# GpSimd in place of VectorE for the low parts of the normalized columns, in the first attention stage of the second layer

## The chip, the cores and the metric

The kernel runs on one core of one Trainium2 chip. The metric is the device time of one execution in microseconds (us). Before the change it is 1368.17 us, the median of 3 runs that lie between 1368.06 and 1368.76.

The engines are named as the profile names them: PE is TensorE (matmuls; PEld its weight loads), DVE is VectorE, ACT is ScalarE, POOL is GpSimd, SP is SyncE, whose queue issues the DMAs.

## The reference

Two blocks, attention and dense, are applied twice to `x` of 2048 rows and 640 columns, all in f32. The two layers use the same weights.

```python
x = x + A(layernorm(x)); x = x + B(layernorm(x))    # layer 1
x = x + A(layernorm(x)); x = x + B(layernorm(x))    # layer 2

def A(x):                       # 32 heads of 20 columns
    q, k, v = split(x @ wqkv)
    pq, pk = q @ w_phi, k @ w_phi                   # per head, 20 by 20
    phi_q = concat([softmax(pq), softmax(-pq)])     # 40 features per head
    phi_k = concat([softmax(pk), softmax(-pk)])
    kv, z = phi_k.T @ v, sum_rows(phi_k)            # per head
    return ((phi_q @ kv) / (phi_q @ z + 1e-6)) @ wo

def B(x):
    h = x @ w1 + b1
    return (h * tanh(softplus(h))) @ w2
```

## The kernel before

**Stages.** Each layer has three stages: `attend_first` (normalized rows to keys, values and queries, and the sums `kva` over all rows), `attend_second` (queries times sums, projection with `wo`), and `dense`. Each stage goes over 8 blocks (`NB`) of 256 rows (`BLK`). The change lies in `attend_first` of the second layer (`layer` is 1), about 713 to 916 us of the profiled execution.

**High and low parts.** A matmul operand is kept as two f32r tiles: the high part is a rounded copy that ScalarE makes, the low part is what the copy left out, source minus high part. Each product is three matmuls: high by high, high by low, low by high (`project_half`, L369 to L375). For the normalized columns the parts are `xth` and `xtl`, made in `Transposed.step` (L302): ScalarE copies (L316, recorded under L132), VectorE subtracts (L317). A block has 5 groups of 128 columns, made in three steps: two of 128x512 (two groups each), one of 128x256.

**Where the columns come from.** In the first layer they are transposed on TensorE into PSUM. In the second, the dense stage has written the normalized rows transposed to memory (`n2_d`); `load_turned` (L350) fetches them into three row tiles `xn` (a pool of 4) and `step` takes source and high part from SBUF.

**The loop of the stage.** For block b the order is keys, values and queries of its two 128-row tiles, k0, k1, v0, v1, q0, q1 (L545). The columns of block b+1 are fetched at the first of these and split at the last three (`nxt.step()`, L574). `features` (L386), for keys and queries, goes round the engines: ScalarE copies out of PSUM, VectorE takes maxima and minima (L400) and subtracts (L401, L403; L401 is GpSimd's for queries), ScalarE takes the exponential (L406), VectorE sums and inverts (L409, L410), GpSimd multiplies (L411). Features of keys go to TensorE (L448); those of queries are transposed by VectorE (L456) and written to memory (`e_d`, L460), which sets their tile `r` free; there are two such tiles, and GpSimd clears part of a tile at its start (L391). The projections share two PSUM tiles `mm`, which ScalarE's copies set free.

**What sets the order.** Outside the parts written by hand, a planner that simulates the program puts the instructions of each engine in order when the kernel is built. ScalarE's are chained in program order (`act`). Each engine runs its instructions in that order, and an instruction that waits holds up those behind it.

**The other users of `Transposed`** are the first layer's first stage, both second stages, and the dense stages; the columns of the second layer's block b0 are made by the dense stage before it (L866).

Of the kernel before, what the change touches and what calls it, by code (L numbers as in the profile page):

```python
# [8 lines left out]
F32 = mybir.dt.float32  # L9
F32R = mybir.dt.float32r  # L10
AF = mybir.ActivationFunctionType
ALU = mybir.AluOpType
# [32 lines left out]
def kernel(  # L45
# [13 lines left out]
    nc = tc.nc  # L59
# [11 lines left out]
    def one_tile():  # L71
        return psum.tile([P, 512], F32, tag="one", name="one", bufs=4)
# [38 lines left out]
    n2_d = [dram.tile([D, BLK], F32, name=f"n2_d{b}") for b in range(NB)]  # L111
# [14 lines left out]
    def act(*args, **kw):  # L126

        if last_act[0] is None or in_written[0]:
            ins = nc.scalar.activation(*args, **kw)
        else:  # L130
            with tc.issue_after(last_act[0]):
                ins = nc.scalar.activation(*args, **kw)  # L132
        last_act[0] = ins.ins
# [143 lines left out]
    def norm_stats(t, xt):  # L277

        bn = work.tile([P, 2, 6], F32, tag="bn", name="bn", bufs=2)
        for c in range(2):  # L280
            nc.vector.bn_stats(bn[:, c], xt[:, t, c * HC:(c + 1) * HC])
        mv = work.tile([P, 2], F32, tag="mv", name="mv", bufs=3)
        nc.vector.bn_aggr(mv, bn)
        return mv

    def norm_scale(b, mvs):

        ve = work.tile([P, BT], F32, tag="ve", name="ve", bufs=2)
        for t in range(BT):
            nc.gpsimd.tensor_scalar(ve[:, t:t + 1], mvs[t][:, 1:2], LN_EPS, 1.0, op0=ALU.add, op1=ALU.mult)  # L290
        nc.gpsimd.tensor_tensor(stats[:, b, 0], ve, neg_half, op=ALU.pow)
        for t in range(BT):
            nc.vector.scalar_tensor_tensor(stats[:, b, 1, t:t + 1], mvs[t][:, 0:1], -1.0,
                                           stats[:, b, 0, t:t + 1], op0=ALU.mult, op1=ALU.mult)

    class Transposed:


        def __init__(self, rows=None, cols=None):
            self.rows, self.cols, self.hs, self.ls = rows, cols, [], []  # L300

        def step(self):  # L302
            c0 = len(self.hs)
            n = min(2, KD - c0)
            if self.rows is None:
                ps = self.cols[c0 // 2]
            else:
                ps = one_tile().rearrange("p (c s) -> p c s", c=2)
                for c in range(n):
                    for t in range(BT):  # L310
                        nc.tensor.transpose(ps[:, c, t * P:(t + 1) * P],  # L311
                                            self.rows[t][:, (c0 + c) * P:(c0 + c + 1) * P], ident)
            nb = 8 if n == 2 else 4
            hi = work.tile([P, n, BLK], F32R, tag=f"xt{n}", name="xth", bufs=nb)
            lo = work.tile([P, n, BLK], F32R, tag=f"xt{n}", name="xtl", bufs=nb)
            act(hi, ps[:, :n], AF.Copy)  # L316
            nc.vector.tensor_tensor(lo, ps[:, :n], hi.bitcast(F32), op=ALU.subtract)  # L317
            for c in range(n):
                self.hs.append(hi[:, c, :])
                self.ls.append(lo[:, c, :])  # L320
# [26 lines left out]
            for q in range(4):  # L347
                nc.sync.dma_start(dst[t, q], rows[t][32 * q:32 * q + 32].rearrange("f (j s) -> f j s", s=32))

    def load_turned(src, tiles):  # L350

        cols = []
        for c, make in zip(range(0, KD, 2), tiles):
            n = min(2, KD - c)
            cols.append(make()[:, :n * BLK].rearrange("p (k s) -> p k s", k=n))
            nc.sync.dma_start(cols[-1], src[c * P:(c + n) * P].rearrange("(k p) s -> p k s", p=P))
        return Transposed(cols=cols)


    def project(xts, t, ws, col, ps=None, w=HC):  # L360
# [53 lines left out]
    def fetch(x_src, b, xt=None):  # L414
        xt = x_tile() if xt is None else xt
        nc.sync.dma_start(xt, row_block(x_src, b))
        return xt

    def attend_first(layer, x_src, first):


        def fetch_normed(b):
            if layer:
                return load_turned(n2_d[b], [row_tile] * 3)
            xt = fetch(x_src, b) if b > 1 else early
            norm_scale(b, [norm_stats(t, xt) for t in range(BT)])
            return xt
# [50 lines left out]
        if first is None:  # L478
            with written():
# [48 lines left out]
                for k in range(KD):  # L528
                    ps = one_tile()
# [13 lines left out]
        for b in range(NB):  # L543
# [14 lines left out]
            for n, (kind, t) in enumerate(order):  # L558
                t = int(t)
                i = b * BT + t  # L560
                if b == 0 and n == (1 if layer else 3):
                    if layer == 0:
                        fold_phi(kv_ws, bd, raw)
                    kva = one_tile()
                    nc.vector.memset(kva[:, :360], 0.0)
                if b == NB - 1 and n == 3:
                    loaded = {0: load(0)}
                if b + 1 < NB:
                    if n == 0:
                        xt = fetch_normed(b + 1)  # L570
                    elif n == 2:
                        nxt = xt if layer else normed(b + 1, xt)
                    elif n > 2:
                        nxt.step()  # L574
                g = {"k": lambda: keys(xts, i, vs[t]), "q": lambda: queries(xts, i, q0 if i == 0 and not layer else None),
                     "v": lambda: values(xts, i, vs[t])}[kind]()
                next(g)
                advance()
                pending.append(g)
# [180 lines left out]
    def dense(x_src, x_dst, w1s, w2s, first, last):  # L760
# [97 lines left out]
        for i in range(len(steps) + SKEW):  # L858
            if i < len(steps):
                b, pr = steps[i]  # L860
                if pr == 0 and b + 1 < NB:
                    fetch_rows_of(b + 1)
                if pr == 2 and b + 1 < NB:
                    blocks[b + 1] = [fetch(x_src, b + 1), None, None]
                if pr == 3 and (b + 1 < NB or not last):
                    nxt = load_turned(n1_d[b + 1] if b + 1 < NB else n2_d[0], (v_tile, v_tile, row_tile))  # L866
                acts[i] = hidden(b, pr)
                if pr == 1 and b + 1 < NB:
                    with tc.issue_after(exps[0]):
                        normalize(b + 1, ahead, ahead)  # L870
                    spill_turned(ahead, n1_d[b + 1])
                if b == 0 and pr == n_pr - 2:
                    with tc.issue_after(exps[0]):
                        nxt.step()
                if pr == n_pr - 1 and (b + 1 < NB or not last):
                    if b + 1 < NB:
                        blocks[b + 1][1] = nxt
                    with tc.issue_after(exps[0]):
                        nxt.all()
# [15 lines left out]
    with tc.block(schedule_with_timeline_sim=True):  # L895
        src, first = x, None
        for layer in range(LAYERS):
# [41 lines left out]
            src = dst  # L939
# [38 lines left out]
```

## Time and profile before

| | us |
|---|---|
| median of 3 runs | 1368.17 |
| profiled execution | 1368.56 |
| its span | 1366.8 |
| PE busy | 1351.2 |
| DVE busy | 1075.5 |
| ACT busy | 578.4 |
| POOL busy | 452.6 |

The profile is of one execution, whose own time is 1368.56 us; its span, 1366.8 us, runs from the first to the last recorded work. In the rows of the timeline the first number is the start in us from the beginning of the span, the second the duration in us, then engine, line, operation and tiles; a bracket at the end gives the idle time of the engine before it and what ended it. In the groups by line, the number behind `x` is the count, then busy us and mean ns of one. In the list of waits stand total us, how often, and the longest. Issuing DMAs is not counted as busy.

### The profile page before, as it was taken

To read this page: it belongs to the slowest core of one execution; us is meant where nothing else is said; L and a number is where in the kernel's file an instruction comes from. 1 tells how busy PE (TensorE), PEld (TensorE's weight loads), DVE (VectorE), ACT (ScalarE), POOL (GpSimd) and SP (SyncE) were. 2 spreads that over 40 slices of the span, in tenths; PEclk is the share of its full clock that TensorE was granted. 3 is DMA by queue.
4 is the path that set the end of the run, shared out by engine and by line. 5 is a ranking of instruction groups with operands and counts; after the bars stand their busy time and mean duration, and the time that the engine had idled before them with its cause. 6 is when DMAs were issued, how large, how long until landed. Compare 5 with 4: busy or idle time off the path is not lost. (4 is left out here: it accounts for less than half of the span.)

```text
span 1366.8 us, 30959 instructions
## 1 busy us (share of the span) xinstructions
PE 1351.2 (99%) x12896; PEld 1337.9 (98%) x12896; DVE 1075.5 (79%) x1822; ACT 578.4 (42%) x970; POOL 452.6 (33%) x401
## 2 busy tenths in 40 slices
PE   9999999999999999999999999999999999999998
PEld 9999999999999999999999999999999999999998
DVE  6888988876787888778769898989668776677775
ACT  5444444212454544455444333432235444444443
POOL 2355554434222222122235444544252211111112
PEclk9999999999999999999999999999999999999999
DMA  9533333798714443334563433458974221333200
GB/s 343 150 81 64 74 60 78 213 282 273 223 36 93 116 117 84 57 94 113 151 218 75 83 60 70 86 132 267 287 251 136 78 71 35 90 97 97 77 21 20
DMA packets 350469, 169.19 MB, mean 124 GB/s; under 512 B 287209, under 2 KB 323801, under 8 KB 350329
## 3 DMA queue, kind: packets, MB, share of 16 engines
q1 hardware_dynamic: 350329, 167.22, 45.4%
q8 instruction: 101, 1.65, 0.5%
q14 instruction: 39, 0.32, 0.1%
HBM read 104.59 MB, written 62.59 MB: 122 GB/s over the span
## 5 line engine op out<-in xcount | busy, mean ns | idle before, releaser
L816 PE MATMUL mm<-r2h,ol 128*128 128x320 f32 x1280 | 304.9, 309 | 0.0
L800 POOL TENSOR_TENSOR ol<-big,ol 128x512 fp32r<-128x512 f32 (+1 forms) x98 | 131.2, 1338 | 477.2 <-ACT ol L799 419.1
L774 PE MATMUL one<-xtl,r1h 128*128 128x256 f32 x960 | 268.2, 279 | 0.0
L774 PE MATMUL one<-xth,r1l 128*128 128x256 f32 x960 | 268.0, 279 | 0.0
L774 PE MATMUL one<-xth,r1h 128*128 128x256 f32 x960 | 265.9, 279 | 0.0
L816 PEld LDWEIGHTS mm<-r2h,ol 128*128 128x128 f32 x1280 | 219.2, 188 | 0.0
L816 PE MATMUL mm<-r2l,ol 128*128 128x320 f32 x640 | 197.3, 309 | 0.0
L375 PE MATMUL mm<-r1h,xth 128*128 128x304 f32 (+1 forms) x600 | 185.4, 309 | 2.2 <-DVE r1l L262 1.5
L375 PE MATMUL mm<-r1h,xtl 128*128 128x304 f32 (+1 forms) x600 | 183.6, 307 | 2.0 <-DVE xtl L317 1.8
L375 PE MATMUL mm<-r1l,xth 128*128 128x304 f32 (+1 forms) x600 | 183.8, 306 | 0.0
L774 PEld LDWEIGHTS one<-xtl,r1h 128*128 128x128 f32 x960 | 180.4, 188 | 0.0
L774 PEld LDWEIGHTS one<-xth,r1l 128*128 128x128 f32 x960 | 180.4, 188 | 0.0
L774 PEld LDWEIGHTS one<-xth,r1h 128*128 128x128 f32 x960 | 179.6, 188 | 0.0
L789 DVE TENSOR_SCALAR big<-big 128x512 f32<-128x512 f32 (+1 forms) x98 | 56.9, 581 | 110.2 <-ACT big L787 110.0
L411 POOL TENSOR_TENSOR r<-r,r 128x1280 f32<-128x1280 f32 x32 | 79.1, 2473 | 131.7 <-DVE r L410 124.1
L816 PEld LDWEIGHTS mm<-r2l,ol 128*128 128x128 f32 x640 | 120.2, 188 | 0.0
L791 ACT ACTIVATE big<-big,two 128x512 f32<-128x512 f32 (+1 forms) x98 | 70.2, 716 | 116.2 <-DVE big L790 116.2
L787 ACT ACTIVATE big<-one,b1s 128x256 f32<-128x256 f32 x192 | 80.9, 468 | 88.8 <-PE one L774 88.3
L799 ACT ACTIVATE ol<-big 128x512 fp32r<-128x512 f32 (+1 forms) x98 | 60.9, 622 | 134.5 <-DVE big L798 134.4
L375 PEld LDWEIGHTS mm<-r1h,xth 128*128 128x128 f32 x600 | 112.8, 188 | 3.9 <-DVE r1l L262 1.7
L375 PEld LDWEIGHTS mm<-r1h,xtl 128*128 128x128 f32 x600 | 112.7, 188 | 2.7 <-DVE xtl L317 2.7
L375 PEld LDWEIGHTS mm<-r1l,xth 128*128 128x128 f32 x600 | 112.8, 188 | 0.1
(136 smaller groups left out, 3125.0 us busy)
## 6 DMA issues: line engine op xcount, KB each, us to landing
e_d<-r SPq DMA_DIRECT2D x128, 160.0 KB, 4.0
big<-e_d SPq DMA_DIRECT2D x32, 640.0 KB, 7.4
x_d<-xt SPq DMA_DIRECT2D x23, 640.0 KB, 4.6
xt<-x_d SPq DMA_DIRECT2D x22, 640.0 KB, 5.5
n_d<-xn SPq DMA_DIRECT2D x176, 80.0 KB, 2.2
xt<-in_x SPq DMA_DIRECT2D x16, 640.0 KB, 4.0
xn<-x_d SPq DMA_DIRECT2D x28, 320.0 KB, 4.4
v<-n_d SPq DMA_DIRECT2D x30, 256.0 KB, 3.0
```

The costliest lines, as they stand in the source:

```text
L375: nc.tensor.matmul(ps[:, :w], a[:, sl], r, start=(k == 0 and n == 0), stop=(k == KD - 1 and n == 2))
L411: nc.gpsimd.tensor_tensor(eg, eg, r.unsqueeze(2).to_broadcast([P, 2 * H, DH]), op=ALU.mult)
L774: nc.tensor.matmul(ph[:, j, :], l, r, start=(n == 0), stop=(n == 3 * KD - 1))
L787: exps[0] = nc.scalar.activation(part(ta, 0)[:, j - js.start], ph[:, j, :], AF.Exp, bias=b1s[:, 2 * pr + j:2 * pr + j + 1]).ins
L789: nc.vector.tensor_scalar_min(e, e, E_CAP)
L791: nc.scalar.activation(r, n, AF.Ln, bias=two)
L799: nc.scalar.activation(ah[:, js], n, AF.Copy)
L800: nc.gpsimd.tensor_tensor(al[:, js], n, ah[:, js].bitcast(F32), op=ALU.subtract)
L816: nc.tensor.matmul(pys[t][:, c, :HC], l[:, j, sl], r, start=(f == 0 and n == 0), stop=(f == KF - 1 and n == 2))
```

## The change

`Transposed` takes the engine that makes its low parts as an argument, VectorE by default. `load_turned` passes it on. In `attend_first`, `fetch_normed`, which in the second layer loads the columns of blocks b1 to b7, asks for GpSimd. That is 21 subtractions: 14 of 128x512 and 7 of 128x256. All other users keep VectorE.

```diff
-        def __init__(self, rows=None, cols=None):
-            self.rows, self.cols, self.hs, self.ls = rows, cols, [], []
+        def __init__(self, rows=None, cols=None, low=nc.vector):
+            self.rows, self.cols, self.low, self.hs, self.ls = rows, cols, low, [], []
...
-            nc.vector.tensor_tensor(lo, ps[:, :n], hi.bitcast(F32), op=ALU.subtract)
+            self.low.tensor_tensor(lo, ps[:, :n], hi.bitcast(F32), op=ALU.subtract)
...
-    def load_turned(src, tiles):
+    def load_turned(src, tiles, low=nc.vector):
...
-        return Transposed(cols=cols)
+        return Transposed(cols=cols, low=low)
...
-                return load_turned(n2_d[b], [row_tile] * 3)
+                return load_turned(n2_d[b], [row_tile] * 3, nc.gpsimd)
```

The planner puts the 21 subtractions into GpSimd's queue. In a steady block that queue then reads (numbers of tiles left out):

```
L411 TensorTensor r<-r,r 128x1280          multiply, q0 of the block before
L317 TensorTensor xtl<-xn,xth 128x512      first subtraction
L411 TensorTensor r<-r,r 128x1280          multiply, q1 of the block before
L411 TensorTensor big<-big,r 128x1280      multiply, k0
L317 TensorTensor xtl<-xn,xth 128x512      second subtraction
L391 Memset r 128x32                       start of q0's tile
L317 TensorTensor xtl<-xn,xth 128x256      third subtraction
L411 TensorTensor big<-big,r 128x1280      multiply, k1
L401 TensorTensor r<-r,m 128x32x20         subtraction of the maxima, q0
```

On VectorE the 21 are gone, and a few neighbours change places: in a steady block the transpose of q0's features (L456) goes behind L401 of k1 and the sum of q1's features (L409), and the extrema of the next k0 (L400) go ahead of L403 of q1. On TensorE three L448 groups and one matmul of the last query move by some places. On SP one load of a last part of the query features (L613) goes one place ahead. ScalarE's order is the same.

## The prediction

> **What bounds the kernel now.** I read the page first, then the stage that is changed in stretches, then what TensorE waits for in it, and last the rows of the engines of one block. The stage runs from about 713 to 916 us: eight blocks of 256 rows, which I number b0 to b7.
>
> ```profile
> span 1366.8 us, 30959 instructions
> PE 1351.2 (99%) x12896; PEld 1337.9 (98%) x12896; DVE 1075.5 (79%) x1822; ACT 578.4 (42%) x970; POOL 452.6 (33%) x401
> ...
> 713.00:916.00 203.00, 200.23 (x2272) 196.67 (x2270) 184.79 (x203) 77.47 (x112) 96.68 (x69) 1.00 0.42 80
> ```
>
> The stretches give length, then PE, PEld, DVE, ACT and POOL busy, the granted clock, the DMA share and GB/s. TensorE has work for 200.23 of 203.00 us, at full clock; VectorE is close behind with 184.79; GpSimd has 96.68. A gain can only come out of the stalls of TensorE, and these are few:
>
> ```profile
> PEld mm L375 <- DVE xtl L317: 2.7, 3, 1.8
> PEld one L448 <- POOL big L411: 1.0, 1, 1.0
> PEld mm L375 <- ACT r L132: 0.8, 2, 0.6
> ...
> 780.22 0.30 PE L375 MATMUL mm<-r1l,xth 128*128 128x304 f32 x1
> 782.11 0.41 PE L375 MATMUL mm<-r1h,xtl 128*128 128x304 f32 x1 [1.59 <-DVE xtl L317]
> ...
> 864.34 0.30 PE L375 MATMUL mm<-r1h,xtl 128*128 128x304 f32 x1
> 866.68 1.47 PE L448 MATMUL one<-big,v 128*21 128x40 f32 x128
> ```
>
> These are waits of the weight loads from 713 to 917 us: total, times, longest. The low parts `xtl` hold TensorE up three times, 2.7 us in all; the longest is seen as the jump from 780.22 to 782.11, where matmuls otherwise start 0.14 apart. In later blocks the same use (864.34) comes without a wait.
>
> **The change part by part.** Twenty-one subtractions (b1 to b7, three each: two of 128x512, one of 128x256) leave VectorE and join GpSimd. The copies `xth`, the matmuls and the DMAs stay as many as they were; in the changed program the matmuls keep their order but for a few places of L448, and one DMA (L613) is issued one place earlier.
>
> ```profile
> L317 DVE TENSOR_TENSOR xtl<-xn,xth 128x512 fp32r<-128x512 f32 x14 | 16.7, 1194 | 0.0
> L317 DVE TENSOR_TENSOR xtl<-xn,xth 128x256 fp32r<-128x256 f32 x7 | 11.1, 1583 | 0.6 <-ACT xth L132 0.6
> ...
> L800 POOL TENSOR_TENSOR ol<-big,ol 128x512 fp32r<-128x512 f32 x94 | 126.1, 1342 | 466.3 <-ACT ol L799 412.6 <-issue 53.7
> L162 POOL TENSOR_TENSOR r1l<-raw,r1h 128x256 fp32r<-128x256 f32 x2 | 1.5, 737 | 0.0
> ```
>
> VectorE gets rid of 16.7 + 11.1 = 27.8 us, 3.9 a block. GpSimd takes on the same subtraction at the price of its rows: 14 x 1.342 + 7 x 0.737 = 23.9 us, 3.4 a block, which lifts it from 96.68 to about 121 of 203 us: room enough, so what counts is the order in its queue. I follow one steady block; first VectorE, then GpSimd, ScalarE:
>
> ```profile
> 849.06 1.51 DVE L456 STREAM_TRANSPOSE r<-r 128x1280 f32<-128x1280 f32 x1 [0.81 <-POOL r L411]
> 850.49 0.78 DVE L401 TENSOR_TENSOR big<-big,m 128x640 f32<-128x640 f32 x1
> 851.20 1.48 DVE L409 TENSOR_REDUCE r<-r 128x64 f32<-128x1280 f32 x1
> 852.59 0.81 DVE L403 TENSOR_TENSOR big<-m,big 128x640 f32<-128x640 f32 x1
> 853.32 0.54 DVE L410 RECIPROCAL r<-r 128x64 f32<-128x64 f32 x1
> 853.78 1.43 DVE L409 TENSOR_REDUCE r<-big 128x64 f32<-128x1280 f32 x1
> 855.13 1.80 DVE L317 TENSOR_TENSOR xtl<-xn,xth 128x512 fp32r<-128x512 f32 x1
> 857.32 1.45 DVE L456 STREAM_TRANSPOSE r<-r 128x1280 f32<-128x1280 f32 x1
> 860.06 0.67 DVE L317 TENSOR_TENSOR xtl<-xn,xth 128x512 fp32r<-128x512 f32 x1
> 862.51 1.47 DVE L317 TENSOR_TENSOR xtl<-xn,xth 128x256 fp32r<-128x256 f32 x1
> ...
> 846.27 2.75 POOL L411 TENSOR_TENSOR r<-r,r 128x1280 f32<-128x1280 f32 x1 [4.89 <-DVE r L410]
> 854.01 2.37 POOL L411 TENSOR_TENSOR r<-r,r 128x1280 f32<-128x1280 f32 x1 [4.99 <-DVE r L410]
> 857.04 0.16 POOL L391 MEMSET r<- 128x32 f32 x1 [0.65 <-DMA e_d<-r]
> 857.54 2.37 POOL L411 TENSOR_TENSOR big<-big,r 128x1280 f32<-128x1280 f32 x1 [0.35 <-DVE r L410]
> ...
> 851.55 0.62 ACT L132 ACTIVATE xth<-xn 128x512 fp32r<-128x512 f32 x1
> 855.94 0.62 ACT L132 ACTIVATE xth<-xn 128x512 fp32r<-128x512 f32 x1
> 859.01 0.41 ACT L132 ACTIVATE xth<-xn 128x256 fp32r<-128x256 f32 x1
> 865.21 0.69 ACT L132 ACTIVATE r<-mm 128x608 f32<-128x608 f32 x1 [5.80 <-DMA e_d<-r]
> ```
>
> See the subtraction of 855.13: 1.80 us, where that of 860.06 takes 0.67. GpSimd's multiply runs from 854.01 to 856.38 just then, and 856.38 plus some 0.6 is the end of it. So a two-input operation of VectorE waits for a running one of GpSimd, and 846.27 (2.75 in place of 2.37, beside VectorE's own work) shows the other direction. The Trainium skill, "SBUF — State Buffer", section "SBUF: two separate sides", states the same as an exclusive lock on a port pair held for the whole instruction, by VectorE operations with two SBUF inputs too; the trace agrees (1.80 against 0.67).
>
> Now the same block in the changed program's order, the lock counted, TensorE and ScalarE kept where they are. On VectorE the transpose of 849.06 goes behind the reduction of 851.20: L401 waits for GpSimd until 849.0 and ends at 849.8, the reduction at 851.2, the transpose at 852.65. The first `xth` is ready at 852.2; GpSimd, idle since 849.0, subtracts from 852.2 to 853.5. L403 waits for that, 853.5 to 854.2, then the reciprocal to 854.7: the cost of the lock on the other side, some 0.85 us. GpSimd's second multiply: 854.8 to 857.2. VectorE's next transpose follows at 857.2, against 857.32 before: what the lock costs, the vanished 1.80 pays. GpSimd goes on with its third multiply, 857.2 to 859.6, the second subtraction to 860.9, the memset (it waits for the DMA of the transpose that is now 2.1 later, so 859.1 in place of 857.04), the third subtraction 860.9 to 861.7, its fourth multiply 861.7 to 864.1. TensorE needs the third low part at 864.34 (before, it came at 862.51 + 1.47 = 863.98, 0.36 ahead; now 2.6 ahead), the second at 864.34 - 6 x 0.14 = 863.5, and the fourth multiply's result at 866.68 (2.6 ahead). ScalarE's copy of 865.21, which waits for the DMA of the transpose of 857.32, stays where it is and ends 0.8 before TensorE has need of its bank at 866.7. So in a steady block no wait appears, and the spare time of the low parts grows.
>
> The boundaries at which TensorE waits before, and the one with the least room:
>
> ```profile
> 722.49 1.28 POOL L401 TENSOR_TENSOR r<-r,m 128x640 f32<-128x640 f32 x1 [11.45 <-DVE m L400]
> 726.43 0.41 PE L375 MATMUL mm<-r1h,xtl 128*128 128x304 f32 x1
> 749.86 0.16 POOL L391 MEMSET r<- 128x32 f32 x1 [0.54 <-POOL big L411]
> 753.66 0.30 PE L375 MATMUL mm<-r1h,xtl 128*128 128x304 f32 x1
> 775.62 2.37 POOL L411 TENSOR_TENSOR big<-big,r 128x1280 f32<-128x1280 f32 x1 [1.15 <-DVE r L410]
> ```
>
> At 726.43 the third subtraction stands behind L401 on GpSimd: 723.8 to 724.5, in time. At 753.66 it stands behind the memset of 749.86 and a multiply: 750.0 + 2.4 + 0.7 = 753.1, in time by 0.6. At 782.11 it stands behind the multiply of 775.62, a subtraction and a memset: 778.0 + 1.3 + 0.7 = 780.0, against a need at 780.36; that multiply moves earlier by up to 1.1, as VectorE loses a subtraction of the 1.8 kind ahead of it. The third wait lies in b3, where the queue has the steady order already. So all three waits go: -2.7.
>
> What is late next is the end of the stage:
>
> ```profile
> 902.11 1.78 DVE L401 TENSOR_TENSOR big<-big,m 128x640 f32<-128x640 f32 x1
> 914.03 2.37 POOL L411 TENSOR_TENSOR big<-big,r 128x1280 f32<-128x1280 f32 x1 [0.66 <-DVE r L410]
> 916.45 0.83 PE L448 MATMUL one<-big,v 128*21 128x40 f32 x64 [0.83 <-POOL big L411]
> ```
>
> Block b7 makes no low parts. TensorE waits 1.0 there (weight loads) for a chain of VectorE and GpSimd which holds one lock wait (1.78, where the same L401 took 0.78 at 850.49). VectorE enters it a little earlier; the gain lies between 0 and 1.0. I take 0.4, nearer to the lower end, since the copy out of PSUM that starts this chain is TensorE's own pace. The wait for ScalarE's `r` (0.8) hangs on a DMA landing and I leave it.
>
> Sum: -2.7 - 0.4 = -3.1 us. The profiled execution took 1368.56 us (span 1366.8 and 1.8 around it): 1365.5. The median of the runs is 0.4 lower, 1368.17: 1365.1.
>
> **The rivals.** 0.2% is 2.7 us, about what a measurement of this kernel can tell from no change.
>
> *All waits go.* If the lighter VectorE also ends the waits for L411 and `r`: -2.7 - 1.0 - 0.8 = -4.5, 1363.7. For it: both are ends of VectorE's queue. Against: a landing sets the one, TensorE's pace the other.
>
> *The chain follows on its own pace.* TensorE comes 2.7 earlier to the end of the stage, but the chain behind 914.03 does not, since DMA landings and locks, not TensorE, pace it: then the gain becomes wait at 916.45, and only some 0.4 is left, 1367.8. For it: VectorE's 184.79 of 203. Against: ScalarE's copies of the projections in every block start on TensorE.
>
> *GpSimd's slower instruction decides.* The Trainium skill, "GPSIMD Engine Reference", section "4.1 Engine selection", puts elementwise work on VectorE, GpSimd being about twice as slow with two inputs; the rows agree (1342 against 670 without the lock). As a mechanism from rows: each of the three waits grows by 0.737 - 0.41 = 0.33, +1.0, 1369.2. Against: VectorE's real price with the lock was 1194 and 1583.
>
> *Slower: the queue of GpSimd.* The third subtraction now stands behind a memset that waits for a DMA landing and behind multiplies that wait for VectorE. If that queue runs x us later than I drew it, five steady boundaries wait x - 2.6 each and b1's x - 0.6. Slower by 2.7 needs 6x - 13.6 = 5.4, x = 3.2; at x = 4 the new waits are 10.4, the old 2.7 gone: 1375.9. Against: the landing came 6.5 us after the transpose in this block and would have to come after 9.
>
> **How the numbers follow.** Forecast 0.48, all waits 0.12, own pace 0.22, slower instruction 0.06, queue 0.12. The forecast lies just past the 0.2% line, so 0.08 of it counts as no change: faster 0.40 + 0.12 = 0.52, same 0.08 + 0.22 + 0.06 = 0.36, slower 0.12. The range from 1363.6 to 1368.0 takes in the first three cases and leaves 0.18 out; the forecast alone spans 1364.4 to 1366.0.
>
> **What would show it.** Right: `xtl` from GpSimd near 1.3 and 0.7 us; no wait of TensorE for `xtl` between 713 and 895; VectorE under 165 busy us in 203; the wait at L448 still there, shorter. Wrong: TensorE waiting for `xtl` of GpSimd in steady blocks, or a wait at the end of the stage that has grown by what was saved.

## The result, and the profile after

| | before | after |
|---|---|---|
| median, 12 runs each | 1369.22 us | 1366.78 us |
| lowest to highest | 1368.06 to 1370.67 | 1366.02 to 1369.84 |
| profiled execution | 1368.56 | 1366.02 |

The ratio of after to before is 0.9981, with a 95% interval of 0.9973 to 0.9988: faster by some 2.4 us, a little under the 0.2% line of the prediction (2.7 us) and clear of no change. The two profiled executions stand 2.54 us apart; 3.1 was forecast. The median of the kernel before is 1369.22 with twelve runs, 1.05 above the 1368.17 of three from which the forecast was counted.

From the page of the changed kernel, span and busy time:

```profile
span 1364.2 us, 30958 instructions
PE 1350.1 (99%) x12896; PEld 1337.3 (98%) x12896; DVE 1057.0 (77%) x1801; ACT 578.2 (42%) x970; POOL 472.2 (35%) x422
```

The changed stage as one stretch (length, then busy time of PE, PEld, DVE, ACT, POOL, the granted clock, DMA share, GB/s):

```profile
713.00:914.00 201.00, 200.32 (x2335) 197.57 (x2335) 166.67 (x182) 77.87 (x113) 118.13 (x91) 1.00 0.44 82
```

VectorE has 18.1 us less to do (184.79 to 166.67), GpSimd 21.4 more (96.68 to 118.13). Neither is a gain in itself. The gain lies in the waits of the weight loads, here between 700 and 930 us (total, times, longest):

```profile
PEld one L311 <- issue: 0.8, 1, 0.8
PEld one L448 <- POOL big L411: 0.6, 1, 0.6
...
PEld mm L375 <- ACT r L132: 0.5, 1, 0.5
```

No wait for `xtl` is left, where there were three of 2.7 us in sum. The one at the end of the stage (L448) went from 1.0 to 0.6, that for ScalarE's `r` from 0.8 to 0.5. Together 3.4 us. L311 is the next stage's: 0.3 before, 0.8 now, so 0.5 is given back there.

To see where the time goes, I set the start of the same matmul of both traces side by side, counting matmuls from the first. Differences to before in us (negative is earlier), at places named by their time in the trace of before:

```
place in before     716.2  748.6  777.1  785.6  807.9  813.3  864.8  914.9  916.9  938.4    end
changed kernel       0.44   0.06  -0.22  -2.07  -2.08  -2.59  -2.61  -2.63  -3.03  -2.56  -2.56
```

The changed kernel enters the stage 0.44 late and leaves it 3.03 early: 3.5 gained, next to the 3.4 of the waits. The steps are where the waits were: 1.85 at 782, 0.5 at 809, 0.4 at 916; the first wait is part of the 0.7 before 777. From 813 to 915 nothing moves.

The subtractions on GpSimd, grouped by shape in the stage (count, then busy us and mean ns):

```profile
L317 POOL TENSOR_TENSOR xtl<-xn,xth 128x512 fp32r<-128x512 f32 x14 | 19.1, 1364 | 23.8 <-ACT xth L132 23.8
L317 POOL TENSOR_TENSOR xtl<-xn,xth 128x256 fp32r<-128x256 f32 x7 | 5.2, 738 | 0.3 <-ACT xth L132 0.3
```

And a steady block of the changed kernel, cuts from the timelines of GpSimd, VectorE and TensorE; times are about 2.6 us earlier than in the trace of before:

```profile
849.63 1.52 POOL L317 TENSOR_TENSOR xtl<-xn,xth 128x512 fp32r<-128x512 f32 x1 [3.83 <-ACT xth L132]
851.11 2.37 POOL L411 TENSOR_TENSOR r<-r,r 128x1280 f32<-128x1280 f32 x1
...
855.77 1.30 POOL L317 TENSOR_TENSOR xtl<-xn,xth 128x512 fp32r<-128x512 f32 x1
...
857.08 0.75 POOL L317 TENSOR_TENSOR xtl<-xn,xth 128x256 fp32r<-128x256 f32 x1
...
849.22 0.78 DVE L403 TENSOR_TENSOR big<-m,big 128x640 f32<-128x640 f32 x1
...
861.73 0.30 PE L375 MATMUL mm<-r1h,xtl 128*128 128x304 f32 x1
```

The third low part is ready at 857.83, and TensorE first uses it at 861.73: 3.9 us of room, as I call the time from a result to its first use, where 0.36 stood in the trace of before. Over the blocks b1 to b7 that use them, the room is 2.9, 0.7, 2.8, 2.4, 3.6, 3.9 and 3.9 us (an expectation below takes 1.2 for b1).

### The profile page after: what moved, and what is told of

Same layout as the page of the kernel before. It is cut to its first block, busy times and chain, and to the rows that moved or that the text cites. A ratio compares the mean times of both kernels' runs of the same rounds, so it can differ in the third digit from the quotient of the medians.

```text
span 1364.2 us, 30958 instructions
## 1 busy us (share of the span) xinstructions
PE 1350.1 (99%) x12896; PEld 1337.3 (98%) x12896; DVE 1057.0 (77%) x1801; ACT 578.2 (42%) x970; POOL 472.2 (35%) x422
## 4 chain that ended last, share of the span: by engine, by line
PE 83%; DVE 3%; DMA 2%; POOL 1%; ACT 0%; issue 0%; SPq 0%; DVEq 0%; ACTq 0%; POOLq 0%
PE one L774 25%; PE mm L816 24%; PE mm L375 17%; PE one L375 11%; PE mm L652 3%; PE one L311 2%; DMA e_d<-r 1%; PE one L448 1%; DVE r L409 1%; DVE r L456 1%; DVE big L401 1%; DVE m L400 1%; DMA raw<-in_wo 0%; DMA v<-in_wv 0%; SPq L460 0%
```

## The experiments

In every kernel that computes a subtraction twice the second run writes the same values over the first, so nothing of the output changes. Ratios are to the kernel before, with 95% intervals; edits are against the changed kernel unless said otherwise. Differences in matmul starts are again those to the trace of before.

| kernel | what differs | ratio |
|---|---|---|
| the change | | 0.9981 [0.9973, 0.9988] |
| e1 | only the third subtraction of a block on GpSimd | 1.0026 [1.0014, 1.0038] |
| e2 | only the first two | 0.9976 [0.9966, 0.9985] |
| e3 | only block b3 | 0.9996 [0.9986, 1.0006] |
| f1 | only the third, only from b3 on | 0.9997 [0.9987, 1.0006] |
| e6 | the dense stage's low parts too | 0.9974 [0.9962, 0.9985] |
| f3 | the first subtraction done twice | 0.9998 [0.9988, 1.0007] |
| f2 | the third done twice | 1.0230 [1.0210, 1.0250] |
| e4 | all three done twice | 1.0236 [1.0221, 1.0251] |
| g1 | subtractions held behind the multiplies of `r` | 0.9991 [0.9981, 1.0000] |
| g2 | f2's work, held behind | 1.0186 [1.0163, 1.0210] |
| g3 | e4's work, held behind | 1.0225 [1.0209, 1.0241] |
| h1 | g2, and k's extrema behind q's reciprocal | 1.0129 [1.0099, 1.0159] |

### One part alone: e1 and e2

```diff
-            self.low.tensor_tensor(lo, ps[:, :n], hi.bitcast(F32), op=ALU.subtract)
+            (self.low if n == 1 else nc.vector).tensor_tensor(lo, ps[:, :n], hi.bitcast(F32), op=ALU.subtract)
```

That is e1; e2 has `n == 2` in place of `n == 1`.

> Only the third subtraction of each block (7 of 128x256) is GpSimd's; the 14 of 128x512 are VectorE's again. Theory A (what counts is when the third low part is ready, since all three waits of TensorE before were for it): the waits at the first keys' projection of b1, b3 and b4 go, 2.2 to 2.7 us, so the ratio to before is 0.998 to 0.9985. Theory B (the gain goes with the busy time that VectorE sheds): 11.1 of 27.8 us are shed, so 0.4 of 2.6 us, 1.0 us, ratio 0.9992.

> Only the first two subtractions of each block (14 of 128x512) are GpSimd's; the third is VectorE's. Theory A: VectorE reaches the third about 2.5 us earlier in a block (1.80 + 0.67 of the first two are gone), while it was late by 1.7, 0.4 and 0.3 us, so the waits go although the awaited instruction is not moved: -2.2 to -2.7 us, ratio 0.998 to 0.9985. Theory B: 16.7 of 27.8 us shed, 1.6 us, ratio 0.9989. Rival C (only the engine of the third one matters, since there it waits for the lock of GpSimd's multiply, 1.5 us each): no gain, waits for the low parts stay near 2.7 us.

e2 is as fast as the whole change, although the low part that TensorE waited for stays on VectorE. Its VectorE timeline at the block of the longest wait:

```profile
774.24 1.51 DVE L456 STREAM_TRANSPOSE r<-r 128x1280 f32<-128x1280 f32 x1 [0.61 <-POOL r L411]
...
777.29 0.78 DVE L317 TENSOR_TENSOR xtl<-xn,xth 128x256 fp32r<-128x256 f32 x1 [0.17 <-ACT xth L132]
778.00 0.54 DVE L410 RECIPROCAL r<-r 128x64 f32<-128x64 f32 x1
```

Without the two subtractions ahead of it, VectorE comes to the third one at 777.29 and is done with it at 778.07; before, it was done at 782.06, where the prediction put the need at 780.36. So the wait goes when the third low part is early enough, and not because GpSimd makes it. From b3 to b7 it has 3.2 us of room and more in e2.

e1 took the same waits away, as was expected (the start of matmuls goes from 6.05 late to 4.20 late at 782 and by another 0.5 at 809) but lost 6.7 us ahead of that, between 749 and 777, so that it is slower than before. Its waits of weight loads:

```profile
PEld mm L375 <- ACT r L132: 5.0, 2, 4.7
```

The timeline of e1 ahead of the longer one, VectorE, GpSimd and ScalarE:

```profile
738.25 0.54 DVE L410 RECIPROCAL r<-r 128x64 f32<-128x64 f32 x1
...
739.39 0.53 DVE L410 RECIPROCAL r<-r 128x64 f32<-128x64 f32 x1
739.84 2.53 DVE L403 TENSOR_TENSOR big<-m,big 128x640 f32<-128x640 f32 x1
742.29 2.85 DVE L317 TENSOR_TENSOR xtl<-xn,xth 128x512 fp32r<-128x512 f32 x1
745.07 1.50 DVE L456 STREAM_TRANSPOSE r<-r 128x1280 f32<-128x1280 f32 x1
...
738.93 5.67 POOL L411 TENSOR_TENSOR r<-r,r 128x1280 f32<-128x1280 f32 x2 [2.87 <-DVE r L410]
...
753.34 0.68 ACT L132 ACTIVATE r<-mm 128x608 f32<-128x608 f32 x1 [9.08 <-DMA e_d<-r]
```

Here the planner put the reciprocal of q0's features behind the sum of q1's. Both reciprocals come close together, GpSimd runs its two multiplies of `r` back to back (738.93 to 744.60), and two of VectorE's two-input operations take 2.53 and 2.85 us beside them, where the same took 0.81 and 0.67 in the trace of before without a neighbour. The transpose behind them starts at 745.07 (741.49 before), its tile is free 3.4 us later, ScalarE's copy of the next `r` starts at 753.34 (749.91 before), and TensorE waits 4.7 us for the bank. The change itself does not do this: at this place its two reciprocals start at 736.65 and 740.31, its two multiplies at 737.34 and 741.00, and the transpose at 741.45. What e1 shows is a second path in the same stage: the loop of the query tile `r`, from reciprocal to multiply to transpose to DMA to the next copy. It had 0.8 us of waits before.

### One block alone, and less of the third: e3 and f1

```diff
-                return load_turned(n2_d[b], [row_tile] * 3, nc.gpsimd)
+                return load_turned(n2_d[b], [row_tile] * 3, nc.gpsimd if b == 3 else nc.vector)
```

That is e3. f1 has e1's line, and `b > 2` in place of `b == 3`, so that VectorE keeps b1 and b2, where e1 had lost.

> GpSimd makes the low parts of one block alone, b3 (3 of the 21 subtractions). Theory A: the one wait of 1.8 us at b3's first keys' projection goes, and those at b1 (0.4) and b4 (0.5) stay or shift by what the order changes: -1.5 to -2.1 us, ratio 0.9985 to 0.9989. Theory B: 3 of 21, -0.4 us, ratio 0.9997.

> Only the third subtraction, and only of b3 to b7, is GpSimd's (5 of 128x256); VectorE does all else. It leaves out what went wrong when all seven thirds were moved: there a wait of 4.7 us for ScalarE's copy of r at b2's keys, before b3. Theory A (readiness of the third low part): the waits at b3 and b4 go, 1.8 + 0.5, the one at b1 stays: -2.0 to -2.4 us from 716 to 925 us, ratio 0.9982 to 0.9986. Theory B (VectorE's shed time): 7.9 of 27.8 us shed, -0.7 us. Rival R (any move of a third disturbs the loop of the r tiles): a wait for r of some us at a later block, slower than before.

```
place in before     716.2  748.6  777.1  785.6  807.9  813.3  864.8  914.9  916.9  938.4    end
e3                   1.60   1.60   1.53  -0.33   0.27   0.85   0.85   0.83   0.96   1.97   2.21
f1                   0.95   0.96   0.32  -1.53  -1.54  -2.05  -2.05  -2.08  -1.07  -0.44   0.00
```

e3 takes 1.86 us away at the one block that it touches, which is the wait of 782. Then it gives 1.2 back: 0.6 by a wait for ScalarE's `r`, and 0.6 in the next block's low part, where the wait grew from 0.5 to 1.1, since TensorE comes earlier and VectorE's subtraction there does not. Another 1.0 goes at L311 (1.3 us of wait), so that the ratio, 0.9996, lies above the 0.9985 to 0.9989 expected and shows no gain; the gain of the one wait is seen in the matmul starts alone. The waits of its weight loads between 795 and 870 us:

```profile
PEld mm L375 <- DVE xtl L317: 1.1, 1, 1.1
```

f1 gains 3.0 us from 716 to 915 with five subtractions moved, more than the 2.0 to 2.4 expected, but 1.0 of it is gone at the end of the stage and another 1.1 behind it (from -1.07 to 0.00), and the ratio, 0.9997, shows no gain. The longest of the waits of its weight loads:

```profile
PEld one L448 <- POOL big L411: 2.0, 1, 2.0
```

The last multiply of the stage in f1's timeline:

```profile
912.97 2.36 POOL L411 TENSOR_TENSOR big<-big,r 128x1280 f32<-128x1280 f32 x1 [1.22 <-DVE r L410]
```

TensorE is there 2.08 us earlier than before, GpSimd's multiply only 1.06 (914.03 before), and the difference is wait. That is the prediction's rival of the chain that keeps its own pace, seen in a near relative of the change. In the changed kernel the same multiply starts 3.02 earlier:

```profile
911.01 2.36 POOL L411 TENSOR_TENSOR big<-big,r 128x1280 f32<-128x1280 f32 x1 [0.66 <-ACT r L132]
```

f1 leaves VectorE 16 of the 21 subtractions, two of each block up to the last among them; that these are what keeps the chain late was not tried by itself.

### More off VectorE: e6

```diff
-                    nxt = load_turned(n1_d[b + 1] if b + 1 < NB else n2_d[0], (v_tile, v_tile, row_tile))
+                    nxt = load_turned(n1_d[b + 1] if b + 1 < NB else n2_d[0], (v_tile, v_tile, row_tile), nc.gpsimd)
```

> As the changed kernel, and GpSimd also makes the low parts that the dense stages load turned (n1_d, and n2_d of b0): 45 more subtractions, 30 of 128x512 and 15 of 128x256, 28 us of VectorE's time without the lock. Theory A: TensorE never waits for a low part in the dense stages, so nothing is to be gained there: within 1 us of the changed kernel, unless GpSimd's own low parts (ol) come late. Theory B: another 2 us faster or more.

VectorE's busy time over the whole kernel falls to 1044.4 us, 12.6 under the changed kernel's (some 28 without the lock were expected); the time is the changed kernel's within the intervals. In the stage it gains 3.3 (from -0.28 at 716 to -3.62 at 917), the same as the change, and it gives 1.4 back at L311. Time taken off VectorE is worth nothing here beyond the waits that end with it.

### What the queue of GpSimd bears: e4, f2, f3

```diff
-            self.low.tensor_tensor(lo, ps[:, :n], hi.bitcast(F32), op=ALU.subtract)
+            for _ in range(2 if self.low is nc.gpsimd else 1): self.low.tensor_tensor(lo, ps[:, :n], hi.bitcast(F32), op=ALU.subtract)
```

That is e4. f2 doubles with the condition `and n == 1` (the third), f3 with `and c0 == 0` (the first).

> As the changed kernel, but GpSimd makes each of the 21 low parts twice over, 23 us of added work for it, 2.0 us before a block's third low part is ready and 1.3 after its first half. Theory A with the room that the changed kernel's trace shows (third low part ready 2.4 to 3.9 us before TensorE needs it in b3 to b7, 1.2 in b1, 0.7 in b2): no wait in b3 to b7, under 1 us in all at b1 and b2, so time within 1 us of the changed kernel. Rival (GpSimd's queue is tight, every subtraction in it is paid for): waits at every boundary, 7 x 2.0 = 14 us less the room, some 5 us or more, slower than before.

> As the changed kernel, but each third subtraction is done twice by GpSimd, 7 x 0.73 = 5.1 us of added work. The planner then puts the first subtraction of most blocks ahead of both multiplies of r, where it waits for its high part. Theory Q (what sits at the head of GpSimd's queue holds up the loop of the r tiles: multiply, transpose, DMA, ScalarE's copy, TensorE's bank): TensorE waits for ScalarE's copy of r at those 4 or 5 blocks, 2 us or more each, 8 to 25 us slower than the changed kernel. Theory L (added busy time counts): at most 5.1 us slower. Theory A alone, with a room of 2.4 us or more for the third: no change.

> As the changed kernel, but each first subtraction is done twice by GpSimd, 7 x 1.30 = 9.1 us of added work, and here the planner leaves the multiply of the first r tile ahead of it, the second run behind the multiply of the second. Theory Q: no wait for r in b3 to b7; the third low part is 1.3 later with a room of 2.4 or more, so within 1 us of the changed kernel. Theory L: 5 to 9 us slower than the changed kernel.

f3 puts 9.1 us more into GpSimd's queue (seven subtractions of 1.3) and costs some 2 us against the change; f2 puts 5.2 us there (seven of 0.738) and costs some 34. So it is not the amount of work that decides. Expected were within 1 us for f3 and e4, and 8 to 25 for f2. The waits of weight loads for ScalarE's copy of `r`, from 714 to 930 us. In f3:

```profile
PEld mm L375 <- ACT r L132: 2.0, 2, 1.0
```

In f2:

```profile
PEld mm L375 <- ACT r L132: 22.0, 10, 3.2
```

In e4 they are 22.4 us, again in ten waits. And GpSimd's timeline of a steady block of e4:

```profile
840.06 1.29 POOL L317 TENSOR_TENSOR xtl<-xn,xth 128x512 fp32r<-128x512 f32 x1 [11.39 <-ACT xth L132]
841.31 5.28 POOL L411 TENSOR_TENSOR r<-r,r 128x1280 f32<-128x1280 f32 x2
```

The low parts cost next to nothing in all three (0.8 us of waits for `xtl` in e4, none in the others): it is again the loop of the query tile, and TensorE waits for it up to twice in a block. e4's rows gave a reason: the first subtraction of the block stands at the head of the queue and waits 11.39 us for its `xth`, and both multiplies of `r` stand behind it. f2 has the same row with 12.12 us of waiting.

### That reason tested: g1, g2, g3

```diff
-            self.low.tensor_tensor(lo, ps[:, :n], hi.bitcast(F32), op=ALU.subtract)
+            if self.low is nc.gpsimd:
+                with tc.issue_after(last_mul[0]):
+                    for _ in range(2 if n == 1 else 1): nc.gpsimd.tensor_tensor(lo, ps[:, :n], hi.bitcast(F32), op=ALU.subtract)
+            else:
+                nc.vector.tensor_tensor(lo, ps[:, :n], hi.bitcast(F32), op=ALU.subtract)
...
-        nc.gpsimd.tensor_tensor(eg, eg, r.unsqueeze(2).to_broadcast([P, 2 * H, DH]), op=ALU.mult)
+        ins = nc.gpsimd.tensor_tensor(eg, eg, r.unsqueeze(2).to_broadcast([P, 2 * H, DH]), op=ALU.mult)
+        if pool_sub: last_mul[0] = ins.ins
```

The last multiply of a query's features is remembered, and the subtractions go behind it in GpSimd's queue. This is g2; g1 has `range(1)`, g3 `range(2)`.

> As the changed kernel, but each subtraction of GpSimd is planned behind the multiply of the last r tile, so that from b3 on both multiplies of r stand ahead of the first subtraction (in the changed kernel it stands between the two). Theory Q: the loop of the r tiles gains room, which the changed kernel did not need, since TensorE waits for r only once there (0.5): within 1 us of the changed kernel, no wait for a low part as the third one keeps over 1 us of room.

> The work of the kernel with the third subtraction doubled (1.023 of before), with the one difference in GpSimd's queue that the first subtraction stands behind both multiplies of r. Theory Q (it was the first subtraction, waiting for its high part at the head of the queue, that held up the r loop): the 22 us of waits for r fall under 5, the time to within 3 us of the changed kernel. Rival T (it was the second run of the third subtraction, between the two subtractions of the maxima of r, or the added work): still 20 us or more slower than the changed kernel.

> The work of the kernel with every subtraction doubled (1.0236 of before, 23 us of added GpSimd work), again with all subtractions behind both multiplies of r. Theory Q: the waits for r fall from 22 to under 5 us; the second multiply of k is now 5.2 us behind the multiplies of r, so some waits at L448 may stay (6.2 before); time within 8 us of the changed kernel. Rival T: still 25 us or more slower.

The reason fell. With no subtraction ahead of the multiplies, g2 keeps 18.0 us of these waits and g3 23.8; they lie 28 and 33 us behind the change, past the marks of rival T, which names where the work was added but not how it costs. Nor does the change gain from the new place: g1 has 1.9 us of waits for `r` and ends at before's time within the interval, or some 1 to 2 us behind the change, where within 1 was expected. The weight loads' waits of g2, whose lines stand 4 to 5 higher:

```profile
PEld mm L379 <- ACT r L132: 18.0, 10, 2.6
```

The timeline of a steady block of g2, VectorE and GpSimd (L413 is the sum, L414 the reciprocal, L415 the multiply, L404 the extrema):

```profile
827.05 1.48 DVE L413 TENSOR_REDUCE r<-r 128x64 f32<-128x1280 f32 x1
828.44 1.53 DVE L404 TENSOR_REDUCE m<-big 128x32 f32<-128x640 f32 x2
829.89 0.81 DVE L407 TENSOR_TENSOR big<-m,big 128x640 f32<-128x640 f32 x1
830.62 1.48 DVE L413 TENSOR_REDUCE r<-r 128x64 f32<-128x1280 f32 x1
832.02 0.54 DVE L414 RECIPROCAL r<-r 128x64 f32<-128x64 f32 x1
...
832.71 5.67 POOL L415 TENSOR_TENSOR r<-r,r 128x1280 f32<-128x1280 f32 x2 [10.85 <-ACT big L132]
```

The sum of q0's features is ready at 828.5, its reciprocal starts at 832.02: four operations in three rows stand between them on VectorE, and the multiplies then run back to back as in e1. In the changed kernel one operation stands between, and the reciprocal starts 2.1 us after the sum starts (840.61 and 842.74), here 5.0. VectorE's order, which the planner sets anew for each program, differs in this between the cheap kernels and the dear ones (f2, e4, g2, g3). From all the traces, the time from the start of q0's sum to the start of its reciprocal, in the blocks of the stage one after the other:

```
before         3.6 2.1 2.1 2.1 2.1 2.1 2.1
the change     3.6 2.1 2.1 2.1 2.1 2.1 2.1
e2, e3, f1     as the change
e6             2.1 in all
g1             as the change
f3             3.6 2.1 2.9 2.9 2.9 2.9 2.1
e1             5.0 3.6 2.9 2.1 2.1 2.1 2.1
e4             5.0 5.0 5.0 5.0 5.0 2.1 3.6
f2, g2         5.0 5.0 5.0 5.0 5.0 5.0 3.6
g3             5.0 5.0 5.0 5.0 5.0 5.0 5.0
```

Where 5.0 stands, time is lost: in nearly every block of the dear kernels, and in the one block of e1 that it lost in. That alone shows no cause, since the planner sets the order of the other engines anew as well.

### VectorE's order: h1

h1 is g2 with the extrema of k held behind the reciprocal of q's features. Its work is that of g2, but the planner changes places on GpSimd and TensorE with it.

```diff
+            if second[0] and not pool_sub and last_rec[0] is not None:
+                with tc.issue_after(last_rec[0]):
+                    nc.vector.tensor_reduce(m[:, s], eh[:, 1], axis=AX.X, op=op)
+            else:
                 nc.vector.tensor_reduce(m[:, s], eh[:, 1], axis=AX.X, op=op)
...
-        nc.vector.reciprocal(r, r)
+        rec = nc.vector.reciprocal(r, r)
+        if pool_sub: last_rec[0] = rec.ins
```

> The same work and the same GpSimd queue as the kernel before it in this list (third subtraction twice, all GpSimd subtractions behind the second multiply of r), but k's extrema are held behind the last reciprocal of q's features, so that on VectorE the reciprocal of q0 stands ahead of the extrema of k1, as it does in the changed kernel. Theory V (the 18 to 22 us of TensorE's waits for ScalarE's copy of r come from VectorE's order, in which the reciprocal of q0 stands some 5 us behind its sum): the waits for r fall from 18.0 to under 5 us and the time comes to within 5 us of the changed kernel, at a ratio of 0.998 to 1.002. Rival T (the second run of the third subtraction keeps GpSimd from the first subtraction of q0's features, whatever VectorE's order): the waits for r stay above 12 us and the ratio stays above 1.012. In between: both have a share.

Its waits of weight loads:

```profile
PEld mm L379 <- ACT r L132: 11.2, 5, 3.4
```

The timeline of VectorE in a steady block of h1 (L417 sum, L418 reciprocal, L406 extrema of k, L409 the subtraction of the maxima):

```profile
822.90 1.48 DVE L417 TENSOR_REDUCE r<-r 128x64 f32<-128x1280 f32 x1
824.30 0.82 DVE L409 TENSOR_TENSOR big<-big,m 128x640 f32<-128x640 f32 x1
825.03 0.55 DVE L418 RECIPROCAL r<-r 128x64 f32<-128x64 f32 x1
825.49 1.48 DVE L406 TENSOR_REDUCE m<-big 128x32 f32<-128x640 f32 x2
```

The reciprocal now starts 2.1 us after the sum, in this block and in all but the first, as in the changed kernel. The waits for `r` fall from ten to five, 18.0 to 11.2 us, one in a steady block in place of two, and the two profiled executions stand 11.6 us apart (1393.90 and 1382.32). By the ratios it is less, some 8 of 28 us: h1's profiled execution is the fastest of its four. So the edit takes 8 to 12 us away, and some 16 or more stay. By the expectation this lies in between, where both theories have a share: the ratio is past the mark of rival T (1.012), but the waits are just under its 12 us.

The waits that went are those for q0's copy; the five that are left, 11.2 us, are for q1's, and another 2.6 us more than in the change are lost at the end of the stage (L448's counterpart L459). What holds TensorE there is seen when a block of the changed kernel is laid beside one of h1, with the first matmuls of k0 and of k1 and ScalarE's copy of k0. The changed kernel:

```profile
832.57 0.30 PE L375 MATMUL mm<-r1h,xth 128*128 128x304 f32 x1
...
838.27 0.41 PE L375 MATMUL mm<-r1h,xth 128*128 128x304 f32 x1
...
836.97 0.68 ACT L132 ACTIVATE big<-mm 128x608 f32<-128x608 f32 x1 [1.48 <-PE mm L375]
```

And h1, with ScalarE's copy of q1 and exponential of q0:

```profile
841.42 0.30 PE L379 MATMUL mm<-r1h,xth 128*128 128x304 f32 x1
...
845.01 0.41 PE L379 MATMUL mm<-r1h,xth 128*128 128x304 f32 x1 [1.46 <-ACT r L132]
...
844.28 0.68 ACT L132 ACTIVATE r<-mm 128x608 f32<-128x608 f32 x1 [4.48 <-DMA e_d<-r]
850.03 0.68 ACT L132 ACTIVATE big<-mm 128x608 f32<-128x608 f32 x1 [5.07 <-PE mm L379]
850.60 1.26 ACT L132 ACTIVATE r<-r 128x1280 f32<-128x1280 f32 x1
```

The changed kernel makes the 30 matmuls of k0 in one go and comes to k1, which needs the tile that q1's copy sets free, 5.7 us after k0's start. h1 breaks off k0 after 14 matmuls, just ahead of the first that reads the third low part, and turns to k1: it stands before the tile some 2 us after k0's start and waits. With the changed kernel's order it would have needed the tile at about 847.1 (841.42 + 5.7, an estimate), when q1's copy was done at 844.96. Since k0 is finished later, its copy starts 8.6 us after k0's start in place of 4.4, and the exponential of q0 stands behind that copy on ScalarE, so the loop of the query tile grows too. GpSimd's first subtraction of q0 (844.23) and VectorE's behind it (845.52) are done at 846.35, 4.2 us before that exponential, so they do not hold it. The same break after 14 matmuls is in every block from b3 to b6 of f2, e4, g2, g3 and h1, and in none of these blocks of the other kernels. So two orders changed together in the dear kernels, VectorE's and TensorE's, and h1 put only the first back. No run changes TensorE's order alone; how the rest divides stays open.

## Why the prediction was right, and where it was off

**Direction and place.** The forecast was 1365.1 us, and 1366.78 was measured, inside the range. Of the 1.7 us between them 1.05 is the higher median of the kernel before; the gain is 2.4 in place of 3.1. All three waits for `xtl` went, at the places named (-2.7 forecast). That this is the cause, and not the lighter VectorE, is shown by the matmul starts of e3, which ends one wait by touching one block, by e2, and by e6, which takes more off VectorE and gains no more.

**The tail.** 0.4 was forecast for L448, and 1.0 became 0.6. The reason given, that TensorE's own pace starts this chain, fits the multiply of 911.01, which came 3.02 us earlier. But f1 shows how near the rival was: with part of the subtractions back on VectorE the same chain came only 1.06 earlier and the wait grew to 2.0.

**ScalarE's `r`.** Left at 0.8, it shrank to 0.5. The stage's gain was 3.4 to 3.5 us, not 3.1.

**The steady block.** The prices, 1.342 and 0.737 us, measured 1.364 and 0.738. The room of the third low part is 3.9 us in b6 and b7, not 2.6. The step that failed is the lock: I let GpSimd's first subtraction win it and L403 wait 0.85. In the trace VectorE is early and wins (L403 at 849.22, 0.78 us), and GpSimd's subtraction takes 1.52 instead of 1.30. So the lock costs GpSimd 0.2, and its queue runs some 1.3 us earlier than drawn. The room for the use of 753.66, forecast at 0.6, is 0.7.

**VectorE under 165 us.** It has 166.67 in 201: the saving was priced with subtractions that included their own lock waits (27.8 us), and part of those waits passed to other operations (L401, on average 1.02 us in the stage before, takes 1.27).

**What the sum left out.** Some 0.5 comes back in the next stage, as a wait of L311 that grew from 0.3 to 0.8 and that moves from kernel to kernel (0.2 in f3, 1.7 in e6); another 0.44 the profiled execution had lost before the stage began. 3.5 less these is the 2.54 between the profiled executions. That this comes so near to 3.1 is partly luck: the stage gave more than was forecast, and what was left out took that back.

**The slower case.** The rival through GpSimd's queue was priced at 1375.9, by low parts that come late. Its mechanism was wrong, and its size too small: in the kernels where GpSimd got more to do it cost up to 34 us, and TensorE hardly ever waited for a low part, but up to 23.8 us for the loop of the query tile, which the prediction had only touched, with a wait that it left alone and a copy that "stays where it is". In the changed kernel the planner kept the reciprocal of q0 one operation behind its sum, and k0's matmuls together; e1, with less moved, waited 4.7 us in the one block where the reciprocal stood 5.0 us behind.

**The slower instruction.** At twice VectorE's price the third low part still came earlier, since it no longer stood behind VectorE's other work and locks; and e2 shows that it need not be GpSimd that makes it. The Trainium skill, "GPSIMD Engine Reference", section "4.1 Engine selection", is right on the price per instruction, and the trace agrees (1.30 us against 0.67 without the lock). Here the place in the queue decided.

## What to carry to other kernels

When TensorE waits for the last of a row of small operations, count what stands ahead of that operation on its engine: moving the ones ahead (e2) did as much as moving all. Gains end with the waits that are seen in the stage; time taken off an engine beyond them was worth nothing here. And where a planner orders the program anew, compare the new order along every loop that has little room, not only along the one that is moved: 5 us of work in GpSimd's queue cost 34 us, with a reciprocal put three places later on VectorE and a row of matmuls broken up on TensorE, while 9 us elsewhere in the same queue cost 2.

## What the runs showed of the hardware

**A slower clock after an idle stretch.** After the wait of 4.7 us in e1, TensorE did not go on at full pace. Stretches of e1 (the columns as above; the eighth figure, behind the five busy times, is the granted clock):

```profile
754.00:763.00 9.00, 8.93 (x128) 8.11 (x131) 3.83 (x5) 1.00 (x3) 5.77 (x7) 0.69 0.49 100
763.00:772.00 9.00, 9.00 (x98) 8.94 (x98) 8.21 (x10) 3.98 (x6) 1.17 (x2) 1.00 0.01 2
```

The clock is 0.69 in the mean over the nine microseconds behind the wait and 1.00 again after them. Projection matmuls start 0.25 us apart from 754.49 to 757.53, where they otherwise start 0.14 apart; e1 lost 1.7 us there beside its waits. The Trainium skill, "TensorE: Matmul & The Clock Gate", section "Part 1: The HAM clock gate", gives half rate after at least one idle window of some 3.4 us and full rate after at least one busy window as long. e1 agrees with it: 4.4 us without a matmul, then the slow stretch. A shorter pause did the same in e2, ahead of the stage, where TensorE stood idle for 1.91 us until 697.30; the two stretches from its trace:

```profile
695.20:697.30 2.10, 0.19 (x3) 0.01 (x1) 0.45 (x3) 0.79 (x2) 0.16 (x1) 1.00 0.56 162
697.00:701.00 4.00, 3.70 (x16) 3.71 (x17) 1.99 (x2) 1.92 (x4) 2.98 (x3) 0.62 0.12 49
```

In the trace of before the stretch from 697 to 701 us is at 1.00. So here some 2 us of idle time were enough, less than the window that the Trainium skill names. A longer wait did not always do it: in h1 TensorE stood idle for 3.18 us until 786.19, and the stretch behind is at full clock.

```profile
786.00:790.00 4.00, 3.81 (x41) 3.57 (x42) 2.92 (x4) 0.13 (x1) 1.27 (x1) 1.00 0.18 62
```

What decides between these two is not settled here. In e1 the wait cost 1.7 us on top of itself; in h1 nothing of the kind is seen.

**Two multiplies back to back lock VectorE out.** The rows of e1 show VectorE's two-input operations at 2.53 and 2.85 us beside GpSimd's 5.67 us of multiplies, three to four times the 0.81 and 0.67 of the same operations without a neighbour. Where the multiplies stood apart, in the same place of the changed kernel, one operation took 1.93 and the next 0.76.
